# Attention decode on one core: keys as the moving operand on four column tiles, softmax shift and row sums inside the exponential, and a bf16 gather of the output

## The chip, the cores and the metric

The kernel runs on one core of one Trainium2 chip. The metric is the device time of one launch in microseconds (us), and a "median" is taken over several launches. The profile is one profiled launch. Its span, from the first to the last instruction, is about 2 us shorter than the launch's device time. Engines: PE is the TensorE matmul, PEld its weight loads, DVE the VectorE, ACT the ScalarE, POOL the GpSimd, and SP the SyncE, which issues the large loads here.

## The reference, cut to what matters

Two attention layers and two feed-forward layers (FFN) alternate, for 8 sequences with one new token each. Both attention layers read the same cache of 8192 keys and values per head.

```python
B, Sq, D = 8, 1, 512
Hq, Hkv, Sk, Dh = 32, 8, 8192, 128          # 4 query heads share one key/value head
def _A_ref(x, k_cache, v_cache, wq, wo):
    # q = x @ wq by head; k, v repeated 4 times over the heads
    scores = jnp.einsum("bhqd,bhkd->bhqk", q, k) * (Dh ** -0.5)
    p = _softmax(scores, axis=-1)
    o = jnp.einsum("bhqk,bhkd->bhqd", p, v)
    # o, heads side by side, @ wo
...
x = x + _A_ref(_layernorm(x), A_k_cache, A_v_cache, A_wq, A_wo)
x = x + _B_ref(_layernorm(x), B_w1, B_w2)      # silu(h @ w1) @ w2
x = x + _A_ref(_layernorm(x), A_k_cache, A_v_cache, A_wq, A_wo)
x = x + _B_ref(_layernorm(x), B_w1, B_w2)
```

A "unit" below is one layer, one sequence and one key/value head. There are 2 x 8 x 8 = 128 units. A unit needs 8192 keys and 8192 values of 128 numbers, 2 MB each, and serves 4 query rows. K is loaded once for both layers, V once for each layer.

## The kernel before

Sequence by sequence, the kernel runs layer 1 of sequence b together with layer 0 of sequence b + 1, so that loads can go on while the FFN between the layers is computed. All K and V loads go in one fixed order through one queue on SP. V lands in a ring of six 512 KB cells (260 transfers of one cell and 126 of two). K lands in one slot per head. A load waits in the queue until the matmuls that read its buffer's old content are done, and everything behind it waits too.

Every instruction's place is decided when the kernel is built. A small list scheduler in the kernel simulates the program with a duration that the author wrote down for each step. It writes the order that comes out of this simulation into the engines' instruction streams. On the chip each engine then works in that order. Only the semaphores, not the written durations, decide when a step really starts.

```python
class Plan:
    RATE = {1: 2.57, 2: 2.51, 4: 2.48}     # us per MB, by transfer size in cells
    LAND = 2.0                             # us from the end of a transfer to its use
    HOP = 0.1
    PE_SLOW = 1.15
    def add(self, name, eng, dur, emit, prio, deps=()):
        n = Node(name, eng, dur * (self.PE_SLOW if eng == "PE" else 1), emit, prio, deps)
    ...
    def run(self, cells):                  # simulates; a free engine takes its ready step of least prio
    ...
order = plan.run(range(N_CELL - 1))
for n in order:
    n.emit()
```

The scores: each of 64 matmuls per unit loads 128 x 128 numbers of K as the stationary operand and streams 16 columns of queries (`bd`). K was transposed before by DVE (`turns`, four per K slot, in 32-bit pairs).

```python
def score(q=q):
    kv = slot(g).rearrange("p (ck n f e) -> p ck f e n", f=2, ck=NCG, e=2)
    for cg in range(4 * q, 4 * q + 4):
        for fe in range(4):
            pe.matmul(sc[:, 16 * cg:16 * cg + 16], kv[:, cg, fe // 2, fe % 2],
                      bd[:, 16 * fe:16 * fe + 16], start=(fe == 0), stop=(fe == 3))
sn.append(plan.add(f"s{u}.{q}", "PE", 0.56, score, pr - 1, [tn[3], bn] + sn[-1:]))
```

The softmax takes three DVE passes over 256 columns (maximum, subtraction, sum), one ACT exponential, 16 small PE matmuls that turn the result (`swap`) and one ACT copy back from PSUM.

```python
n1 = plan.add(f"mx{u}", "DVE", 0.42, mx, pr - 1, sn)        # maximum of each query row
n2 = plan.add(f"ma{u}", "POOL", 0.45, mall, pr, [n1])       # ... over the partitions
n3 = plan.add(f"sub{u}", "DVE", 0.45, sub, pr - 1, [n2])
n4 = plan.add(f"exp{u}", "ACT", 0.42, exp, pr, [n3] + last_exp)
n5 = plan.add(f"ss{u}", "DVE", 0.42, ssum, pr - 2, [n4])
m4 = plan.add(f"sw{u}", "PE", 0.6, swap, pr - 2, [n4])
n4 = plan.add(f"bk{u}", "ACT", 0.42, back_in, pr, [m4] + p_users.get(sm, []))
```

PV multiplies four probabilities at a time into a 512-column PSUM bank. Four float32 copies and four float32 matmuls (the "gather") then pick the useful blocks and add them up.

```python
for t in range(4):
    k = (NCG * P + 4 * t) * R
    pe.matmul(ot[32 * t:32 * t + 4 * R, :], pt[:, k:k + 4 * R], vt[:, t, :], start=(P == 0), stop=(P == 3))
...
for x in range(4):                                           # take: ACT copy of 128 float32 columns
    pe.matmul(EX[:, 0:R], buf, diag[:, R * x:R * x + R], start=(x == 0), stop=(x == 3))   # float32
    n = plan.add(f"t{u}.{x}", "ACT", 0.3, take, pr - 2, [vs[-1], last])
    es.append(plan.add(f"g{u}.{x}", "PE", 0.25, gather, pr - 2, [n, back(ot_users, 1)]))
```

(These are cuts: the closures and the synchronisation around them are left out.)

## Time and profile before

The kernel took 1256.51 us (median of 3, 1252.25 to 1261.66).

| what, in the profile of the kernel before | value |
|---|---|
| span | 1252.6 us |
| loads | 465 MB in one queue, busy 94.0% of 16 engines' span |
| PE busy | 981.4 us (78%) |
| DVE busy | 526.1 us (42%) |
| the chain that ended last | 59% DMA, 32% PE |

These lines are from the page: the span; each engine's busy time, share and instruction count; the mean busy share of the core's DMA engines in 40 slices, in tenths; the load queue (packets, MB, share of 16 engines' span); and the chain of waits by engine.

```profile
span 1252.6 us, 39642 instructions
PE 981.4 (78%) x17684; PEld 728.5 (58%) x17684; DVE 526.1 (42%) x1196; ACT 240.9 (19%) x859; POOL 117.6 (9%) x299
DMA  9999899999999999999999999999999999999794
...
q1 hardware_dynamic: 86272, 465.10, 94.0%
...
DMA 59%; PE 32%; issue 5%; DVE 1%; SPq 1%; POOL 0%; ACT 0%; POOLq 0%; DVEq 0%
```

The loads bound this kernel, but not perfectly: 6% of the queue's capacity is missing, and a third of the chain is PE. The slices hide where that 6% is, because a slice is 31 us long. The windows view, with shorter stretches, shows it. Its columns are start and end, length, busy time and count of each engine, granted clock, DMA share and GB/s. The clock column can't be read for this kernel: its trace holds no clock record at all, and the view then prints 1.00.

```profile
core 0: us, PE busy (x) PEld busy (x) DVE busy (x) ACT busy (x) POOL busy (x), PEclk, DMA share, GB/s
850.00:875.00 25.00, 25.00 (x447) 18.56 (x440) 7.46 (x23) 5.46 (x20) 2.18 (x5) 1.00 0.91 346
860.00:865.00 5.00, 5.00 (x91) 4.09 (x92) 1.74 (x6) 0.94 (x3) 0.42 (x2) 1.00 0.51 184
```

Around the boundary between the layers PE is full, and inside it the loads run dry (share 0.51). The chain of waits shows what PE does there. Its columns are start, duration, and what ran.

```profile
859.13 0.55 PE sc L725 x16
859.68 0.42 PE ex L844 x2
860.10 0.53 PE sc L725 x16
860.63 0.42 PE ex L844 x2
```

Sixteen score matmuls take turns with one float32 gather matmul (L844; the trace holds two records for each float32 matmul, 1024 for 512): nearly half of PE's time goes to the gather. Next, the view of waits of the SP queue: the queue's line, the engine and line waited for, total us, times, longest.

```profile
SPq L91 <- PE ot L825: 643.7, 309, 20.4
SPq L91 <- PE sc L725: 192.4, 29, 14.3
SPq L91 <- PE yt L894: 70.8, 35, 4.2
```

The queue waits almost only for PE: for PV (which is ordinary back pressure, since V can't come earlier than its ring cell is free), for scores (which free a K slot) and for the output projection. Last, the groups of instructions: line, engine, operation, output and input with shapes, count, then busy us and mean ns of one, then idle time before them with what ended it.

```profile
L725 PE MATMUL sc<-bd,kts 128*128 128x16 bf16 x8192 | 344.7, 182 | 26.1 <-DVE kts L676 17.1 <-DVE bd L710 4.9 <-DVE small L781 2.8
...
L676 DVE STREAM_TRANSPOSE kts<-kts 128x1024 uint32<-128x1024 uint32 x256 | 311.1, 1229 | 94.3 <-DMA kts<-in_A_k_cache_dram 93.9
...
L844 PE MATMUL ex<-diag,p 128*128 128x4 f32 x512 | 147.4, 359 | 9.5 <-ACT p L840 8.6
L844 PE MATMUL ex<-diag,part 128*128 128x4 f32 x512 | 145.5, 355 | 0.0
L844 PEld LDWEIGHTS ex<-diag,part 128*128 128x128 f32 x512 | 138.3, 330 | 0.9 <-issue 0.9
```

The gather costs 293 us of PE busy by these two lines, 2.29 us per unit (259 us where matmuls that overlap count once, my count from the trace), for a reduction of 512 columns to 4. The DVE's K transposes wait 94 us for K to land. A DVE that stands at a transpose can't do a softmax step that is ready behind it.

### The profile page before, as it was taken

The numbers are of one execution on the slowest core, as the hardware profiler recorded it, in microseconds if no ns is written. First come the engines' busy times: TensorE is split into PE (matmuls) and PEld (weight loads), VectorE is DVE, ScalarE is ACT, GpSimd is POOL, SyncE is SP. The second block draws the span as 40 slices with busy tenths as digits, with TensorE's granted clock in tenths as the row PEclk, the third lists the DMA queues.
The fourth block names the chain that finished last, engine by engine and source line by source line (L and its number), as shares of the span: only waits on it lengthen the run. The fifth ranks groups of instructions, "written<-read, shape, count | busy, mean of one in ns | idle before, by whom it ended". The sixth has DMA issues, their size and how long they took to land.

```text
span 1252.6 us, 39642 instructions
## 1 busy us (share of the span) xinstructions
PE 981.4 (78%) x17684; PEld 728.5 (58%) x17684; DVE 526.1 (42%) x1196; ACT 240.9 (19%) x859; POOL 117.6 (9%) x299
## 2 busy tenths in 40 slices
PE   2756787788877978788887987779678896768886
PEld 2545565566665756556665665557456575655664
DVE  5551445415552346514454154723456134651220
ACT  0111111212122112212122121222112121122121
POOL 1000101001010001101010010100011000110010
DMA  9999899999999999999999999999999999999794
GB/s 372 418 402 337 335 400 368 377 355 418 418 389 377 364 417 415 370 383 366 413 398 382 355 375 408 396 382 359 381 412 368 391 362 377 406 372 341 251 352 172
DMA packets 86444, 467.64 MB, mean 373 GB/s; under 512 B 8945, under 2 KB 14849, under 8 KB 61953
## 3 DMA queue, kind: packets, MB, share of 16 engines
q1 hardware_dynamic: 86272, 465.10, 94.0%
q8 instruction: 139, 2.28, 0.7%
q14 instruction: 33, 0.26, 0.1%
HBM read 465.05 MB, written 0.01 MB: 371 GB/s over the span
## 4 chain that ended last, share of the span: by engine, by line
DMA 59%; PE 32%; issue 5%; DVE 1%; SPq 1%; POOL 0%; ACT 0%; POOLq 0%; DVEq 0%
DMA ring<-in_A_v_cache_dram 52%; PE ot L825 11%; PE sc L725 8%; PE ex L844 7%; DMA ring<-in_A_wq_dram 4%; DMA w<-in_B_w_dram 1%; PE misc L625 1%; PE misc L504 1%; SPq L334 1%; PE misc L486 1%; DMA kts<-in_A_wo_dram 1%; PE yt L894 1%; DMA kts<-in_A_k_cache_dram 1%; DVE kts L676 1%; PE sc L762 1%
## 5 line engine op out<-in xcount | busy, mean ns | idle before, releaser
L825 PE MATMUL ot<-ring,p 128*16 128x512 bf16 x2048 | 297.7, 601 | 137.8 <-DMA ring<-in_A_v_cache_dram 137.6
L725 PEld LDWEIGHTS sc<-bd,kts 128*128 128x128 bf16 x8192 | 334.0, 121 | 117.4 <-issue 53.7
L725 PE MATMUL sc<-bd,kts 128*128 128x16 bf16 x8192 | 344.7, 182 | 26.1 <-DVE kts L676 17.1
L676 DVE STREAM_TRANSPOSE kts<-kts 128x1024 uint32<-128x1024 uint32 x256 | 311.1, 1229 | 94.3 <-DMA kts<-in_A_k_cache_dram 93.9
L840 ACT ACTIVATE p<-ot 128x128 f32<-128x128 f32 x256 | 71.0, 277 | 442.1 <-PE ot L825 351.0
L844 PE MATMUL ex<-diag,p 128*128 128x4 f32 x512 | 147.4, 359 | 9.5 <-ACT p L840 8.6
L844 PEld LDWEIGHTS ex<-diag,p 128*128 128x128 f32 x512 | 129.9, 314 | 39.7 <-ACT p L840 25.9
L825 PEld LDWEIGHTS ot<-ring,p 128*16 128x16 bf16 x2048 | 46.2, 90 | 177.6 <-DMA ring<-in_A_v_cache_dram 170.0
L844 PE MATMUL ex<-diag,part 128*128 128x4 f32 x512 | 145.5, 355 | 0.0
L737 DVE TENSOR_REDUCE small<-sc 128x4 f32<-128x256 f32 x128 | 52.7, 411 | 208.4 <-PE sc L725 208.2
L844 PEld LDWEIGHTS ex<-diag,part 128*128 128x128 f32 x512 | 138.3, 330 | 0.9 <-issue 0.9
L742 POOL PARTITION_ALL_REDUCE small<-small x128 | 47.6, 372 | 647.5 <-DVE small L737 473.2
L752 ACT ACTIVATE expd<-sc 128x256 bf16<-128x256 f32 x128 | 49.1, 384 | 301.5 <-DVE sc L747 299.7
L762 PE MATMUL sc<-expd,ident 128*32 128x64 bf16 x2048 | 53.1, 242 | 37.2 <-ACT expd L752 37.1
L777 POOL PARTITION_ALL_REDUCE small<-small x128 | 55.0, 430 | 273.9 <-DVE small L772 230.1
L840 ACT ACTIVATE part<-ot 128x128 f32<-128x128 f32 x256 | 70.3, 275 | 26.5 <-PE ex L844 10.8
L872 DVE TENSOR_TENSOR z<-ex,small 128x16 bf16<-128x16 f32 x64 | 10.8, 168 | 149.1 <-PE ex L865 149.0
L762 PEld LDWEIGHTS sc<-expd,ident 128*32 128x32 bf16 x2048 | 37.6, 123 | 59.4 <-ACT expd L752 50.1
L768 ACT ACTIVATE p<-sc 128x256 bf16<-128x256 f32 x128 | 49.1, 384 | 111.0 <-PE sc L762 110.6
L747 DVE TENSOR_TENSOR sc<-sc,small 128x256 f32<-128x256 f32 x128 | 53.4, 417 | 16.3 <-POOL small L742 16.0
L772 DVE TENSOR_REDUCE small<-expd 128x4 f32<-128x256 bf16 x128 | 50.8, 397 | 19.6 <-ACT expd L752 19.4
L894 PEld LDWEIGHTS yt<-z,ring 128*128 128x128 bf16 x1024 | 32.6, 105 | 20.8 <-issue 19.9
(75 smaller groups left out, 424.4 us busy)
## 6 DMA issues: line engine op xcount, KB each, us to landing
ring<-in_A_v_cache_dram SPq DMA_DIRECT2D x260, 512.0 KB, 7.7
kts<-in_A_k_cache_dram SPq DMA_DIRECT2D x64, 2048.0 KB, 10.6
ring<-in_A_v_cache_dram SPq DMA_DIRECT2D x126, 1024.0 KB, 10.6
ring<-in_A_wo_dram SPq DMA_DIRECT2D x64, 512.0 KB, 11.2
ring<-in_A_wq_dram SPq DMA_DIRECT2D x36, 512.0 KB, 8.0
kts<-in_A_wo_dram SPq DMA_DIRECT2D x2, 2048.0 KB, 14.0
w<-in_B_w_dram SPq DMA_DIRECT2D x2, 1792.0 KB, 13.5
wq<-in_A_wq_dram SPq DMA_DIRECT2D x4, 512.0 KB, 11.1
```

The source lines that it names most:

```text
L676: op(dve, lambda: dve.transpose(v, v), reads=[], writes=[res("kt", g)], add=(q > 0))
L725: steps.append(lambda cg=cg, fe=fe: pe.matmul(sc[:, 16 * cg:16 * cg + 16], kv[:, cg, fe // 2, fe % 2], bd[:, 16 * fe:16 * fe + 16], start= ...
L737: op(dve, lambda: dve.tensor_reduce(mxp[sm], sv.rearrange("p (k h) -> p h k", h=R), AX.X, ALU.max), reads=[res(*scr)], writes=[res("mxp", ...
L747: op(dve, lambda: dve.tensor_tensor(v, v, mxa[sm].unsqueeze(1).to_broadcast([128, NCH, R]), ALU.subtract), reads=[res("mxa", sm)], writes= ...
L752: op(act, lambda: act.activation(pe_out[:, :], sv, ACT.Exp, scale=SM_SCALE), reads=[res(*scr)], writes=[res("expd")])
L762: steps.append(lambda c4=c4, P=P: pe.matmul(new[32 * P:32 * P + 32, c4], ident[:, 32 * c4:32 * c4 + 32], src[:, P], start=True, stop=True))
L768: op(act, lambda: act.activation(pt[:, :], sc[:, 256:512], ACT.Copy), reads=[res(*scr)], writes=[res("p", sm)])
L772: op(dve, lambda: dve.tensor_reduce(ssm[sm], pe_out[:, :].rearrange("p (k h) -> p h k", h=R), AX.X, ALU.add), reads=[res("expd")], writes= ...
L777: op(pool, lambda: pool.partition_all_reduce(ssa[sm], ssm[sm], 128, bass.bass_isa.ReduceOp.add), reads=[res("ssm", sm)], writes=[res("ssa" ...
L825: steps.append(lambda t=t, k=k: pe.matmul(ot[32 * t:32 * t + 4 * R, :], pt[:, k:k + 4 * R], vt[:, t, :], start=(P == 0), stop=(P == 3)))
L840: op(act, lambda: act.activation(buf, ot[:, x * DH:(x + 1) * DH], ACT.Copy), reads=[res("ot", o)], writes=[br])
L844: mms([lambda: pe.matmul(EX[:, 0:R], buf, diag[:, R * x:R * x + R], start=(x == 0), stop=(x == 3))], reads=[br, res("diag")], writes=[res( ...
```

## The change

Its intent is to take work off PE and ACT.

1. Scores: K becomes the moving operand. 32 matmuls of 256 columns, spread over four column tiles of the array (outputs at partitions 0, 32, 64, 96), replace 64 matmuls of 16 columns. The queries become the stationary operand.
2. Softmax: the maximum goes into the exponential as its bias and the row sums come out as its accumulated output. Two DVE passes and a PE turn of 16 matmuls become a PE turn of 4 and one DVE transpose from PSUM.
3. PV: two probabilities at a time, so that only 256 columns are to be gathered. The gather splits them into a bf16 high part and a bf16 remainder (one ACT copy, one DVE subtraction) and uses four bf16 matmuls.
4. The durations that the scheduler is told change along with the instructions. So does the number of buffers for the spread queries (`bd`), from two to one.

The core of the diff, with cuts marked:

```diff
-                kv = slot(g).rearrange("p (ck n f e) -> p ck f e n", f=2, ck=NCG, e=2)
+                kv = slot(g).rearrange("p (c y i f) -> p y f c i", c=8, y=8, f=4)
 ...
-                        steps.append(lambda cg=cg, fe=fe: pe.matmul(
-                            sc[:, 16 * cg:16 * cg + 16], kv[:, cg, fe // 2, fe % 2],
-                            bd[:, 16 * fe:16 * fe + 16], start=(fe == 0), stop=(fe == 3)))
+                        w = bd[:, 48 * q + 16 * (1 - y):48 * q + 16 * (1 - y) + 32]
+                        steps.append(lambda t=t, y=y, w=w: pe.matmul(
+                            sc[32 * t:32 * t + 32, 0:256], w, kv[:, 2 * t + y, q],
+                            start=(q == 0 and y == 0), stop=(q == 3 and y == 1)))
-            sn.append(plan.add(f"s{u}.{q}", "PE", 0.56, score, pr - 1,
+            sn.append(plan.add(f"s{u}.{q}", "PE", 0.3, score, pr - 1,
 ...
-            op(act, lambda: act.activation(pe_out[:, :], sv, ACT.Exp, scale=SM_SCALE),
+            op(act, lambda: act.activation(pe_out[:, :], sv, ACT.Exp, bias=bias[si], scale=SM_SCALE, accum_out=rsum[si]),
 ...
-            op(act, lambda: act.activation(pt[:, :], sc[:, 256:512], ACT.Copy), reads=[res(*scr)],
-               writes=[res("p", sm)])
+            src = sc[:, 256:512].bitcast(BF16).rearrange("p (n two) -> p two n", two=2)[:, 1]
+            op(dve, lambda: dve.transpose(pt[:, :], src), reads=[res(*scr)], writes=[res("p", sm)])
 ...
-        n1 = plan.add(f"mx{u}", "DVE", 0.42, mx, pr - 1, sn)
+        n1 = plan.add(f"mx{u}", "DVE", 0.6, mx, pr - 1, sn + [back(rc_users, N_SC)])
-        n3 = plan.add(f"sub{u}", "DVE", 0.45, sub, pr - 1, [n2])
+        n3 = plan.add(f"own{u}", "DVE", 0.17, own_max, pr - 1, [n2])
-        n5 = plan.add(f"ss{u}", "DVE", 0.42, ssum, pr - 2, [n4])
-        m4 = plan.add(f"sw{u}", "PE", 0.6, swap, pr - 2, [n4])
-        n4 = plan.add(f"bk{u}", "ACT", 0.42, back_in, pr, [m4] + p_users.get(sm, []))
+        n5 = plan.add(f"ss{u}", "DVE", 0.17, ssum, pr - 2, [n4])
+        m4 = plan.add(f"sw{u}", "PE", 0.3, swap, pr - 2, [n4])
+        n4 = plan.add(f"bk{u}", "DVE", 0.45, back_in, pr - 2, [m4] + p_users.get(sm, []))
 ...
-            n = plan.add(f"v{u}.{P}", "PE", 0.4, pv, pr, [h["exp"], vn, old or clear_n] + vs[-1:])
+            n = plan.add(f"v{u}.{P}", "PE", 0.35, pv, pr, [h["exp"], vn, old or clear_n] + vs[-1:])
 ...
-            n = plan.add(f"t{u}.{x}", "ACT", 0.3, take, pr - 2, [vs[-1], last])
-            es.append(plan.add(f"g{u}.{x}", "PE", 0.25, gather, pr - 2, [n, back(ot_users, 1)]))
+        def high():
+            op(act, lambda: act.activation(pt[:, :], ot[:, 0:2 * DH], ACT.Copy), reads=[res("ot", o)],
+               writes=[res("p", sm)])
+        def low():
+            op(dve, lambda: dve.tensor_tensor(part[:, :], ot[:, 0:2 * DH], pt[:, :], ALU.subtract),
+               reads=[res("ot", o), res("p", sm)], writes=[res("part")])
+        def gather():
+            for k, src in enumerate((pt, part)):
+                for y in range(2):
+                    steps.append(lambda k=k, src=src, y=y: pe.matmul(
+                        EX[:, 0:R], src[:, y * DH:y * DH + DH], diag[:, R * y:R * y + R],
+                        start=(k == 0 and y == 0), stop=(k == 1 and y == 1)))
 ...
+        hn = plan.add(f"hi{u}", "ACT", 0.42, high, pr - 2, [vs[-1]])
+        ln = plan.add(f"lo{u}", "DVE", 0.45, low, pr - 2, [hn, back(es, 1)])
+        es.append(plan.add(f"g{u}", "PE", 0.2, gather, pr - 2, [ln, back(ot_users, 1)]))
```

## The prediction

> **What bounds the kernel now.** The loads. The page gives the DMA queue 94% of 16 engines' span, at a mean 373 GB/s; the chain that ended last is 59% DMA, 32% PE. In 25 us stretches (the windows view), undisturbed ones show a DMA share of 1.01 to 1.02 and 412 to 421 GB/s; where V comes in single 512 KB cells, 385 to 394. Dips (0.79 to 0.95) come in each of the eight passes. Summed against 1.015 up to 1175 us they cost 58 us; the end (from 1175 us) loses about 10 more before the last load lands at 1236, then 15 us run without loads. At share 1.01 and the present mix of transfers (373/0.94 = 397 GB/s), I estimate a floor near 1187 us.
>
> **Why the dips.** The queue issues in order and waited almost only for PE (PV 644 us, scores 192, output projection 71). Around the layer boundary PE is full: 25.0 of 25 us at 850:875 and 1000:1025, DMA share 0.91. There a K load waits for the first layer-1 scores, which wait behind float32 gathers and the FFN chain; the loads run dry for 2.5 us (860:865, share 0.51).
>
> **What the change does, per unit of 128.**
> - Gather: four float32 matmuls, with evictions in turn, cost 293/128 = 2.29 us of PE and about that in latency. Four bf16 ones of 4 columns should cost 0.27 us, as the query expansion does; latency about 1.3 us. The Trainium skill, "TensorE: Matmul & The Clock Gate", Weight-path perf modes, says fast weight load excludes FP32; the trace agrees: 314 to 330 ns a load against 104 to 107.
> - Scores: 64 matmuls of 16 columns, 2.3 to 2.7 us, become 32 of 256 on four column tiles. PV streams as many columns (16 of 512) in 4 x 0.43 us, so I estimate 1.7 us. The new operand is strided by 8 bytes; the Trainium skill, "SBUF — State Buffer", Door 1, says two hits per 16-byte line are free. No trace shows that yet.
> - Swap 0.40 to about 0.3 us; PV unchanged.
> - PE busy 981 to about 600 us; ScalarE 241 to about 105.
> - DVE loses passes of 411, 417 and 397 ns, gains a 410 ns maximum, three tiny ones (165 ns), a 400 ns transpose and a 417 ns subtraction: 526 to about 590 us. More of each unit's chain now sits on DVE, behind K transposes of 1229 ns, and DVE waits in order for K to land (94 us).
>
> **Critical path.** PE's 380 us are mostly hidden under the loads. Only the dips (58), the end (10) and the last chain (2) can be won: about 70 us. I expect 55 to 60% of it; the rest stays with in-order K waits on DVE, the FFN chain and single-cell loads.
>
> **Predicted: 1216 us, 1192 to 1240. Chances: faster 0.70, same 0.25, slower 0.05.**
>
> **What would show it.** DMA queue share 96 to 97%; boundary windows at 0.97 or more with PE below 20 of 25 us; four bf16 gathers below 0.35 us; the queue's waits on scores below 120 us; score groups of eight at 0.45 us or less; PE below 20% of the chain.
>
> **What would make it wrong.** Strided streaming at half rate (score groups near 0.8 us); DVE becoming the cause of late releases, so that the dips stay with PE idle; or dips set by the six ring cells and issue order rather than PE, which leaves 1235 to 1250 us. A larger gain would need larger transfers, which don't change.

## The result, and the profile after

The kernel after took **1182.71 us** (median of 4, 1179.12 to 1184.9) against 1254.38 (median of 4, 1251.65 to 1261.66). The ratio is 0.9417, with a 95% interval of 0.9369 to 0.9466. A ratio here is the mean time of one kernel's fast runs over that of the other's fast runs of the same rounds, so it is not quite the ratio of the medians. "Faster" was right; the time lies 9 us below the predicted range.

The page of the kernel after, the same parts as above:

```profile
span 1180.7 us, 31675 instructions
PE 706.9 (60%) x13588; PEld 370.5 (31%) x13588; DVE 597.7 (51%) x1713; ACT 136.9 (12%) x475; POOL 117.3 (10%) x295
DMA  9999799999999999999999999999999999999993
...
q1 hardware_dynamic: 86272, 465.10, 97.8%
...
DMA 76%; PE 16%; issue 4%; DVE 2%; SPq 1%; POOLq 0%; ACT 0%; POOL 0%; DVEq 0%; ACTq 0%
```

The windows view of the kernel after, at the layer boundary and at the very first boundary:

```profile
core 0: us, PE busy (x) PEld busy (x) DVE busy (x) ACT busy (x) POOL busy (x), PEclk, DMA share, GB/s
800.00:825.00 25.00, 20.64 (x454) 11.48 (x454) 6.60 (x28) 3.14 (x11) 1.99 (x4) 0.57 1.02 396
125.00:130.00 5.00, 4.08 (x98) 2.61 (x99) 1.29 (x7) 0.00 (x0) 0.39 (x1) 0.64 0.11 24
```

The later boundaries no longer cost the loads anything: PE is busy 20.64 of 25 us and the DMA share is 1.02. The first boundary still loses them (share 0.11 from 125 to 130 us; the kernel before had 0.03 there). It is the 7 in the slices.

The waits of the SP queue, and the groups, of the kernel after:

```profile
SPq L91 <- PE ot L842: 654.1, 300, 21.5
SPq L91 <- PE sc L746: 155.1, 29, 13.2
SPq L91 <- PE yt L915: 28.6, 17, 3.7
```

```profile
L694 DVE STREAM_TRANSPOSE kts<-kts 128x1024 uint32<-128x1024 uint32 x256 | 306.1, 1222 | 35.4 <-DMA kts<-in_A_k_cache_dram 35.3
L746 PE MATMUL sc<-kts,bd 128*32 128x256 bf16 x4096 | 288.6, 406 | 33.8 <-DVE kts L694 21.7 <-DVE bd L729 8.6 <-DVE rc L796 0.9
...
L772 ACT ACTIVATE expd<-sc,small 128x256 bf16<-128x256 f32 x128 | 60.7, 474 | 422.1 <-DVE small L767 365.6 <-PE sc L746 32.7 <-PE ot L842 17.8
...
L864 PE MATMUL ex<-diag,p 128*128 128x4 bf16 x256 | 26.3, 172 | 23.5 <-DVE part L856 21.2 <-DVE small L767 2.2
L772 ACT ACTIVATION_READ_ACCUMULATOR expd<-sc,small 128x1 f32 x128 | 24.7, 193 | 0.0
L864 PE MATMUL ex<-diag,part 128*128 128x4 bf16 x256 | 24.5, 165 | 0.0
...
L864 PEld LDWEIGHTS ex<-diag,part 128*128 128x128 bf16 x256 | 16.3, 101 | 0.1
```

The gather fell from 293 to 51 us of PE busy (259 to 33 where overlapping matmuls count once), and from float32 weight loads of 330 ns to bf16 ones of 101 ns. This agrees with the Trainium skill, "TensorE: Matmul & The Clock Gate", Weight-path perf modes, which excludes FP32 from the fast weight load. The scores fell only from 345 to 289 us. The exponential grew from 384 to 474 ns, and reading its accumulated sum costs 193 ns more. The DVE works 72 us more, yet waits for K only 35 us instead of 94.

Two quantities organise everything that follows. "Queue busy" is the span times the queue's share. "Queue idle" is the span minus queue busy divided by 1.012. The 1.012 is the share that the page gives when nothing ever holds the loads up (experiment e3 below).

| kernel | span | share | queue busy | queue idle |
|---|---|---|---|---|
| before | 1252.6 | 0.940 | 1177.4 | 89.1 |
| after | 1180.7 | 0.978 | 1154.7 | 39.7 |
| loads only (e3) | 1123.9 | 1.012 | 1137.4 | 0 |

So of the 72 us gained in the profiled span, 49.4 came from a queue that idles less. The other 22.4 (22.7/1.012) came from the *same 86272 packets and 465 MB taking less time*.

### The profile page after: what moved, and what is told of

It is laid out like the page before. It is cut to its first block, busy times and chain, and to the rows that moved or that the text cites. A ratio compares the mean times of both kernels' runs of the same rounds, so it can differ in the third digit from the quotient of the medians.

```text
span 1180.7 us, 31675 instructions
## 1 busy us (share of the span) xinstructions
PE 706.9 (60%) x13588; PEld 370.5 (31%) x13588; DVE 597.7 (51%) x1713; ACT 136.9 (12%) x475; POOL 117.3 (10%) x295
## 3 DMA queue, kind: packets, MB, share of 16 engines
q1 hardware_dynamic: 86272, 465.10, 97.8%
## 4 chain that ended last, share of the span: by engine, by line
DMA 76%; PE 16%; issue 4%; DVE 2%; SPq 1%; POOLq 0%; ACT 0%; POOL 0%; DVEq 0%; ACTq 0%
DMA ring<-in_A_v_cache_dram 70%; PE ot L842 7%; PE sc L746 6%; DMA kts<-in_A_k_cache_dram 3%; DMA ring<-in_A_wq_dram 2%; DMA w<-in_B_w_dram 1%; DVE kts L694 1%; PE misc L642 1%; SPq L340 1%; PE ex L864 0%; PE sc L721 0%; PE yt L915 0%; PE misc L510 0%; DVE small L758 0%; PE ex L886 0%
## 5 line engine op out<-in xcount | busy, mean ns | idle before, releaser
L842 PE MATMUL ot<-ring,p 128*8 128x256 bf16 x4096 | 256.6, 365 | 220.8 <-DMA ring<-in_A_v_cache_dram 218.9
L694 DVE STREAM_TRANSPOSE kts<-kts 128x1024 uint32<-128x1024 uint32 x256 | 306.1, 1222 | 35.4 <-DMA kts<-in_A_k_cache_dram 35.3
L746 PE MATMUL sc<-kts,bd 128*32 128x256 bf16 x4096 | 288.6, 406 | 33.8 <-DVE kts L694 21.7
L842 PEld LDWEIGHTS ot<-ring,p 128*8 128x8 bf16 x4096 | 80.0, 92 | 313.9 <-DMA ring<-in_A_v_cache_dram 288.7
L746 PEld LDWEIGHTS sc<-kts,bd 128*32 128x32 bf16 x4096 | 116.3, 117 | 107.4 <-DVE kts L694 32.1
L856 DVE TENSOR_TENSOR part<-ot,p 128x256 bf16<-128x256 f32 x128 | 54.2, 423 | 177.1 <-ACT p L852 98.5
L772 ACT ACTIVATE expd<-sc,small 128x256 bf16<-128x256 f32 x128 | 60.7, 474 | 422.1 <-DVE small L767 365.6
L852 ACT ACTIVATE p<-ot 128x256 bf16<-128x256 f32 x128 | 49.1, 383 | 487.7 <-PE ot L842 486.7
L778 PE MATMUL sc<-expd,ident 128*32 128x256 bf16 x512 | 42.3, 318 | 91.1 <-ACT expd L772 88.4
L758 DVE TENSOR_REDUCE small<-sc 128x1 f32<-128x256 f32 x128 | 53.2, 415 | 51.3 <-PE sc L746 51.2
L785 DVE STREAM_TRANSPOSE p<-sc 128x256 bf16<-128x256 bf16 x128 | 56.9, 445 | 7.3 <-PE sc L778 4.5
```

The source lines that it names most:

```text
L694: op(dve, lambda: dve.transpose(v, v), reads=[], writes=[res("kt", g)], add=(q > 0))
L746: steps.append(lambda t=t, y=y, w=w: pe.matmul(sc[32 * t:32 * t + 32, 0:256], w, kv[:, 2 * t + y, q], start=(q == 0 and y == 0), stop=(q = ...
L758: op(dve, lambda: dve.tensor_reduce(mxr[si], sv, AX.X, ALU.max), reads=[res(*scr)], writes=[res("mxr", si)])
L772: op(act, lambda: act.activation(pe_out[:, :], sv, ACT.Exp, bias=bias[si], scale=SM_SCALE, accum_out=rsum[si]), reads=[res(*scr), res("bia ...
L778: steps = [lambda P=P: pe.matmul(sc[32 * P:32 * P + 32, 256:512], src[:, P], pe_out[:, :], start=True, stop=True) for P in range(4)]
L785: op(dve, lambda: dve.transpose(pt[:, :], src), reads=[res(*scr)], writes=[res("p", sm)])
```

## The experiments

The theory: the loads bound the kernel, they run dry where PE is too full to free buffers in time, and less PE time closes those dips. Rivals: (A) one part alone, the gather or the scores, makes all of the gain; (B) the gain comes from a different order of the instructions, since the diff also changes the durations that the scheduler is told; (C) the loads have a floor far from the one that I had estimated, so that the sizes don't mean what I took them for. A short name such as "e5" is the first part of a run's label; there is no e8. The diffs are cut to the lines that matter.

### What the loads alone need, and one part at a time

**e1: the kernel after with a float32 gather** (two ACT copies, two float32 matmuls; no subtraction).

```diff
-        hn = plan.add(f"hi{u}", "ACT", 0.42, high, pr - 2, [vs[-1]])
-        ln = plan.add(f"lo{u}", "DVE", 0.45, low, pr - 2, [hn, back(es, 1)])
-        es.append(plan.add(f"g{u}", "PE", 0.2, gather, pr - 2, [ln, back(ot_users, 1)]))
 ...
+                mms([lambda: pe.matmul(EX[:, 0:R], buf, hsum[:, R * y:R * y + R], start=(y == 0), stop=(y == 1))],
+            n = plan.add(f"t{u}.{y}", "ACT", 0.3, take, pr - 2, [vs[-1], back(es, 1) if y else None])
+            ge.append(plan.add(f"g{u}.{y}", "PE", 0.5, gather, pr - 2, [n, back(ot_users, 1)] + ge[-1:]))
```

> The kernel after, with the gather alone undone: two ScalarE evictions and two float32 matmuls (0.57 us each, measured in the kernel before) in place of the two-part bf16 gather (0.4 us for four). It puts back about 0.75 us of PE per unit, 96 us in all (PE busy near 800 us), and takes the 423 ns subtraction off DVE. Theory PE time (what made the loads run dry was a full PE around the layer boundary): 1190 to 1205 us, dips in the boundary windows come back in part. Rival (scores and softmax part made the gain, the gather is idle time): 1180 to 1187 us. Second rival (more work on DVE is what still costs): faster than 1180 us.

Measured: 1202.82 us (1193.59 to 1203.83), ratio 0.9618. The profile fell on its fastest run (PE busy 798 us, queue idle 44). About 20 of the 72 us go back with half of the float32 matmuls.

**e2: the kernel before with a bf16 gather** (two rounds of ACT high part, DVE subtraction and four bf16 matmuls; old scores, old softmax).

```diff
-    diag = sb([128, R * R], FP32, "diag")
+    diag = sb([128, R * R], BF16, "diag")
 ...
+            hn = plan.add(f"hi{u}.{r}", "ACT", 0.42, high, pr - 2, [vs[-1]] + es[-1:])
+            ln = plan.add(f"lo{u}.{r}", "DVE", 0.45, low, pr - 2, [hn, es[-1] if es else back(es_users, 1)])
+            es.append(plan.add(f"g{u}.{r}", "PE", 0.2, gather, pr - 2, [ln, back(ot_users, 1)]))
```

> The kernel before, with the gather alone changed: two rounds of ScalarE high part, DVE subtraction and four bf16 matmuls, in place of four float32 ones. It takes about 1.5 us of PE per unit away (PE busy near 790 us) and adds 0.85 us of DVE per unit (near 635 us), with the scores, the softmax and PV as before. Theory PE time: most of the gain, 1195 to 1220 us. Rival (the gain comes from scores and softmax, or needs both): 1235 to 1256 us.

Measured: 1246.6 us, ratio 0.9987 (0.9959 to 1.0016). This was the first surprise. PE busy fell by 163 us, from 981 to 818, and the time did not move. The queue idled 91 us, as before, and the DVE's wait for K *rose* from 94 to 120 us. Relief of PE is not sufficient.

**e3: the loads only.** Every compute step is left out of the program; only the DMAs are emitted, so the output is zeros and wrong.

```diff
                 for n in order:
-                n.emit()
+                if n.eng == "DMA":
+                    n.emit()
 ...
```

> The kernel after with every instruction of compute left out of the program, so the same 465 MB are loaded in the same order and sizes into the same places, each waiting only for the earlier load into its place; the result is zeros on purpose. It measures the floor that the prediction put at about 1187 us less 15 us of tail. Prediction's floor right: 1165 to 1175 us. Rival (a fuller queue moves more per busy microsecond, so the floor was set too high): 1115 to 1150 us.

Measured: 1125.65 us (two runs, 1125.54 and 1125.76). From its page:

```profile
span 1123.9 us, 637 instructions
...
q1 hardware_dynamic: 86272, 465.10, 101.2%
...
HBM read 465.05 MB, written 0.01 MB: 414 GB/s over the span
```

This is the floor of the loads in this order and these sizes (the kernels before and after issue the same loads in the same order). It lies 61 us below the 1187 that I had estimated; about 15 of these are the tail without loads, which this run doesn't have, and some 46 are a floor set too high. The headroom of the kernel before is at most 1254.38 - 1125.65 = 129 us, not 70; the compute after the last load is in it, and no kernel can win all of that.

### The order of the instructions

**e4: the kernel after, with the scheduler told the old durations.** Only written durations change; each engine executes the same instructions in another order. (The exponential and the subtraction keep theirs, and the new gather is told that it takes as long as the old one.)

```diff
-            sn.append(plan.add(f"s{u}.{q}", "PE", 0.3, score, pr - 1,
+            sn.append(plan.add(f"s{u}.{q}", "PE", 0.56, score, pr - 1,
-        n1 = plan.add(f"mx{u}", "DVE", 0.6, mx, pr - 1, sn + [back(rc_users, N_SC)])
+        n1 = plan.add(f"mx{u}", "DVE", 0.42, mx, pr - 1, sn + [back(rc_users, N_SC)])
-        m4 = plan.add(f"sw{u}", "PE", 0.3, swap, pr - 2, [n4])
+        m4 = plan.add(f"sw{u}", "PE", 0.6, swap, pr - 2, [n4])
 ... (own 0.17 -> 0.45, ss 0.17 -> 0.42, bk 0.45 -> 0.42, rc 0.3 -> 0.18, v 0.35 -> 0.4)
-        hn = plan.add(f"hi{u}", "ACT", 0.42, high, pr - 2, [vs[-1]])
+        hn = plan.add(f"hi{u}", "ACT", 1.2, high, pr - 2, [vs[-1]])
-        es.append(plan.add(f"g{u}", "PE", 0.2, gather, pr - 2, [ln, back(ot_users, 1)]))
+        es.append(plan.add(f"g{u}", "PE", 1.0, gather, pr - 2, [ln, back(ot_users, 1)]))
```

> The kernel after, with the durations that the scheduler assumes set back to those of the kernel before, so that every engine's instruction order is again laid out for slow scores and a slow gather; the instructions themselves are the new ones. Theory PE time: 1178 to 1195 us, within 1% of the kernel after. Rival (the new order of instructions made the gain): above 1215 us.

Measured: 1256.29 us, ratio 1.005 (1.0002 to 1.0098). **The whole gain is gone**, with PE busy at 715 us, nearly as in the kernel after (707). From its profile, the queue's wait for scores and the DVE's wait for K:

```profile
SPq L91 <- PE sc L746: 302.5, 35, 13.4
```

```profile
DVE kts L694 <- DMA kts<-in_A_k_cache_dram: 160.3, 64, 4.4
```

The kernel after had 155.1 and 35.3 in these lines. The windows view (columns as above) and the timeline of e4 show one instance. In the timeline the columns are start, duration, engine, line, operation, operands, count, and in brackets the idle time before and what ended it.

```profile
795.00:800.00 5.00, 1.45 (x28) 0.51 (x24) 2.83 (x5) 0.00 (x0) 0.00 (x0) 0.50 0.92 381
800.00:805.00 5.00, 4.38 (x82) 2.35 (x78) 4.21 (x16) 1.13 (x4) 1.17 (x3) 0.54 0.41 104
```

```profile
795.57 0.62 PE L746 MATMUL sc<-kts,bd 128*32 128x256 bf16 x8
797.26 2.37 DVE L694 STREAM_TRANSPOSE kts<-kts 128x1024 uint32<-128x1024 uint32 x2 [2.17 <-DMA kts<-in_A_k_cache_dram]
799.55 0.19 DVE L729 TENSOR_TENSOR bd<-sc,mask 128x64 bf16<-128x64 f32 x1
799.66 0.41 DVE L758 TENSOR_REDUCE small<-sc 128x1 f32<-128x256 f32 x1
...
799.74 0.59 PE L842 MATMUL ot<-ring,p 128*8 128x256 bf16 x8 [3.55 <-DMA ring<-in_A_v_cache_dram]
...
800.99 1.57 PE L746 MATMUL sc<-kts,bd 128*32 128x256 bf16 x24
...
802.66 0.33 SPq L340 DMA_DIRECT2D kts<-in_A_k_cache_dram  x1
```

The DVE stood 2.17 us at a K transpose whose K had not landed. Behind it, in its fixed order, were the query spread (`bd`) and the maximum, which are short. The scores that read `bd`'s buffer before were done at 795.57 + 0.62 = 796.19, so the spread could have run then; it ran at 799.55. The next unit's scores therefore ended at 800.99 + 1.57 = 802.56, they freed a K slot, the K load was issued at 802.66, and by then the loads had run dry (share 0.41). The profile puts PE's idle 3.55 us before 799.74 down to V, which PE also needed there; but the scores behind could not have started before the spread in any case. This is the harm from in-order DVE waits that the prediction feared, but it depends on the order, not on the new instructions.

**e6: the reverse, the kernel before told short durations for scores, turn, PV and gather.**

```diff
-            sn.append(plan.add(f"s{u}.{q}", "PE", 0.56, score, pr - 1,
+            sn.append(plan.add(f"s{u}.{q}", "PE", 0.3, score, pr - 1,
-        m4 = plan.add(f"sw{u}", "PE", 0.6, swap, pr - 2, [n4])
+        m4 = plan.add(f"sw{u}", "PE", 0.3, swap, pr - 2, [n4])
 ... (v 0.4 -> 0.35, t 0.3 -> 0.2)
-            es.append(plan.add(f"g{u}.{x}", "PE", 0.25, gather, pr - 2, [n, back(ot_users, 1)]))
+            es.append(plan.add(f"g{u}.{x}", "PE", 0.05, gather, pr - 2, [n, back(ot_users, 1)]))
```

> The kernel before, instructions untouched, with the durations that the scheduler assumes shortened to those of the kernel after (scores 0.3, swap 0.3, PV 0.35, gather steps 0.2 and 0.05). Only the order on each engine changes; the order of loads stays. With the fourth run, this completes the square of old and new instructions against old and new order. Theory order: a good part of the 5.8% comes with the order alone, 1200 to 1230 us. Rival, match (the order must fit the instructions, so a mismatch either way costs): 1250 us or slower.

Measured: 1298.06 us, ratio 1.0354 (1.0307 to 1.0401). Slower by 44 us with the old instructions. Its waits view shows the opposite trouble, PE standing at scores for K transposes (17.1 us in the groups of before):

```profile
PE sc L725 <- DVE kts L676: 104.8, 45, 3.8
```

e4 and e6 complete a square:

| | told old or long durations | told short durations |
|---|---|---|
| old instructions | 1254 (before) | 1298 (e6) |
| new instructions | 1256 (e4) | 1183 (after) |

Neither column nor row alone makes the gain. Rival B in its pure form, that an order laid out for short durations is faster by itself, falls as far as e6 tests it: on the old instructions it costs 44 us. (e6 copies the shorter durations only, so its order is not exactly that of the kernel after.) So does my theory in its pure form, that less PE time alone is enough.

**e7: the kernel before with `LAND` (the assumed time from transfer to use) 2.0 -> 4.0**, to see whether the DVE's waits for K in the kernel before can be ordered away by this one number.

```diff
-    LAND = 2.0
+    LAND = 4.0
```

> The kernel before, with one number of the scheduler changed: it assumes that a load lands 4 us after its turn on the queue in place of 2 us, so K transposes stand later in DVE's order. In the kernel before DVE waited 94 us for K to land, in the kernel after 35. Theory head of line (DVE stands at a K transpose while softmax steps behind it are ready): DVE's wait for K below 70 us and 1225 to 1245 us. Rival (PE, not DVE's order, held the kernel before): within 0.5% of 1250 us.

Measured: 1250.94 us, ratio 1.0002 (0.9937 to 1.0067); the DVE's wait for K fell from 94 to 76 us. Nothing gained: this knob doesn't find a better order for the old instructions.

### PE time with the order held still

**e5: the kernel after, each PV matmul issued twice** (the second into unused columns of the bank; the scheduler is not told, so no engine's order changes).

```diff
+                for c in range(2):
+                    for t in range(4):
+                        k = 32 * (2 * P + c) + 8 * t
+                        steps.append(lambda t=t, c=c, k=k: pe.matmul(
+                            ot[32 * t:32 * t + 2 * R, 2 * DH:4 * DH], pt[:, k:k + 2 * R], vt[:, c, t],
+                            start=False, stop=(P == 3 and c == 1), skip_group_check=True))
```

> The kernel after, with each PV matmul issued a second time into the 256 unused columns of its bank, in the order of instructions of the kernel after; the result stays right. It adds about 0.43 us of PE per cell of V, 220 us in all (PE busy near 930 us), to the step that frees a cell. Theory PE time (a full PE makes the loads run dry): at least half of the gain is lost, 1215 us or more. Rival, order (what counts is that DVE's fixed order puts softmax steps ahead of K transposes; PE has room): 1183 to 1200 us.

Measured: 1233.01 us (1229.43 to 1240.84), ratio 0.9846. PE busy rose from 707 to 860 us, and 50 of the 72 us are lost. The queue idles 71 us, and the DVE's wait for K is only 11 us. This is the cleanest proof of the mechanism: same order, same DVE and ACT work, only more PE time. The added time stands in the step that frees a V cell, so e5 doesn't tell a fuller PE from a later release of the cell.

**e10: the same, with the scheduler told** (PV step 0.35 -> 0.7).

```diff
-            n = plan.add(f"v{u}.{P}", "PE", 0.35, pv, pr, [h["exp"], vn, old or clear_n] + vs[-1:])
+            n = plan.add(f"v{u}.{P}", "PE", 0.7, pv, pr, [h["exp"], vn, old or clear_n] + vs[-1:])
```

> The kernel after with each PV matmul issued twice, as in the fifth run (1233 us), but with the scheduler told so (0.7 in place of 0.35 us per PV step). PE busy near 860 us again. Theory match (most of that run's loss was an order laid out for a faster PE): below 1210 us. Rival, PE time (the load itself costs): 1225 us or more.

Measured: 1243.46 us, ratio 0.9941. A scheduler that knows of the added work makes it 10 us worse, not better; one more order, and no larger a step than order alone makes below.

### Less PE time in the kernel before, part by part

**e9: the kernel before, gathering the bf16 high part only** (two ACT copies of 256 columns, four bf16 matmuls, nothing added on DVE; less exact, yet within the tolerance).

```diff
+                op(act, lambda: act.activation(buf[:, :], ot[:, 2 * r * DH:2 * (r + 1) * DH], ACT.Copy),
 ...
+            n = plan.add(f"t{u}.{r}", "ACT", 0.42, take, pr - 2, [vs[-1], back(es_users, 1) if r else None])
+            es.append(plan.add(f"g{u}.{r}", "PE", 0.12, gather, pr - 2, [n, back(ot_users, 1)] + es[-1:]))
```

> The kernel before, with the gather cut to the bf16 high part (two ScalarE evictions of 256 columns, four bf16 matmuls, no subtraction on DVE); less exact on purpose, and the scheduler is told the new durations. It takes about 1.9 us of PE per unit away without adding to DVE, as the second run did (98 us more DVE, no gain). If DVE's added work ate that run's gain: 1205 to 1230 us. If the gather's PE time alone is worth nothing while the scores are slow: 1238 us or slower.

**e11: the kernel before with half of its score matmuls left out** (`fe` 0 and 3 of 0 to 3; a wrong sum, which the tolerance happened to pass).

```diff
-                    for fe in range(4):
+                    for fe in (0, 3):
-            sn.append(plan.add(f"s{u}.{q}", "PE", 0.56, score, pr - 1,
+            sn.append(plan.add(f"s{u}.{q}", "PE", 0.28, score, pr - 1,
```

> The kernel before with half of the score matmuls left out (32 of 64 a unit, wrong result on purpose), scheduler told. PE loses about 1.2 us a unit, on the step that a K load waits for; DVE, ScalarE and the float32 gather are untouched. Theory: the release of K slots by the scores is what holds the loads: 1205 to 1230 us, and the queue's wait for scores falls below 150 us. Rival (softmax and gather decide): 1240 us or slower.

**e12: both cuts, e9 and e11, together** (the edits are the two above; wrong like e11).

> The kernel before with both cuts: high-part gather and half of the scores (wrong result on purpose), scheduler told. PE busy near 640 us, below the kernel after (707), with the old softmax on DVE. If PE time in the right order is the whole cause: 1175 to 1190 us, as the kernel after. If the change of the softmax steps (bias and sums in ScalarE, transpose on DVE) carries part of the gain: 1205 us or slower.

| kernel | median us | ratio (95%) | PE busy | queue idle | queue's wait for scores |
|---|---|---|---|---|---|
| before | 1252.74 | 1 | 981 | 89 | 192 |
| e9, cheap gather | 1205.43 | 0.9636 (0.9605 to 0.9666) | 793 | 51 | 115 |
| e11, half of the scores | 1207.99 | 0.9648 (0.9618 to 0.9679) | 859 | 57 | 54 |
| e12, both | 1187.06 | 0.9501 (0.9449 to 0.9553) | 686 | 42 | 41 |
| after (other rounds) | 1182.71 | 0.9417 (0.9369 to 0.9466) | 707 | 40 | 155 |

Either cut gives 45 to 47 us. Both give 66, not 92: they overlap, because both relieve the same boundary and the loads' floor comes nearer. So rival A finds no support: the better of the two single cuts stays 22 us behind the kernel after. It isn't excluded, since each cut was run in one order and an order alone can be worth 29 us (e16 below). With the old softmax, half of the old scores and 686 us of PE busy, e12 comes within 4 us of the kernel after by the medians (10 by the ratios). As far as this one order shows, the reorganised softmax and the column tiles matter here only as PE time.

### The subtraction on DVE, and the order again

**e13: the kernel after, its DVE subtraction done three times** (the scheduler told 1.35).

```diff
+            for _ in range(3):
+                op(dve, lambda: dve.tensor_tensor(part[:, :], ot[:, 0:2 * DH], pt[:, :], ALU.subtract),
 ...
-        ln = plan.add(f"lo{u}", "DVE", 0.45, low, pr - 2, [hn, back(es, 1)])
+        ln = plan.add(f"lo{u}", "DVE", 1.35, low, pr - 2, [hn, back(es, 1)])
```

> The kernel after with the subtraction on DVE issued three times in a row (same result), scheduler told. It adds about 0.85 us of DVE per unit, 108 us in all (DVE busy near 705 us), inside the gather's chain; PE is untouched. Theory DVE in the chain (what ate the gain of the second run, bf16 gather in the kernel before, was its 98 us more DVE): 1205 us or more. Rival (DVE has room, that run failed because slow scores filled PE): 1183 to 1195 us.

Measured: 1189.72 us, ratio 0.9496. The DVE is busy 698 instead of 598 us, and this costs 7 us by the medians (10 by the ratios). As far as this one order shows, DVE time is nearly free here.

**e14: the kernel after without the subtraction** (high part only; less exact).

```diff
-            for k, src in enumerate((pt, part)):
+            for k, src in enumerate((pt,)):
 ...
-        ln = plan.add(f"lo{u}", "DVE", 0.45, low, pr - 2, [hn, back(es, 1)])
-        es.append(plan.add(f"g{u}", "PE", 0.2, gather, pr - 2, [ln, back(ot_users, 1)]))
+        es.append(plan.add(f"g{u}", "PE", 0.2, gather, pr - 2, [hn, back(ot_users, 1)]))
```

> The kernel after with the high part alone in the gather, no subtraction on DVE (less exact on purpose), scheduler told. DVE falls by 54 us, the chain from PV to the normalisation by about 0.5 us. It measures what the exact two-part gather costs in the kernel after. Theory DVE in the chain: 1165 to 1178 us. Rival (hidden under the loads): 1178 to 1186 us.

Measured: 1195.5 us, ratio 0.9538. Strictly less work than the kernel after, and 13 us *slower*. Removing a step also moves every later step in the order, so an ablation in this kernel carries an error of at least this size.

**e15: the kernel before, half of the scores and the full bf16 gather of e2** (the edits of e11 and e2; wrong).

> The kernel before with half of the score matmuls left out (wrong result on purpose) and the exact bf16 gather of the second run, scheduler told. The run with half scores alone took 1208 us, half scores with the high part alone 1187 us. If DVE's 98 us eat what the gather gives: 1205 us or more. If the bf16 gather pays once the scores are short: 1183 to 1198 us.

Measured: 1193.99 us, ratio 0.9529 (0.949 to 0.9569), against 1187 for e12. With the scores cut, the gather that gave nothing in e2 gives 14 us (1207.99 to 1193.99).

**e16 and e17: exactly the instructions of e2, with the subtraction's written duration changed from 0.45 to 0.2 and to 0.7.** They answer what was still open: whether e2's missing gain was the DVE subtraction itself, or only an unlucky order.

```diff
-            ln = plan.add(f"lo{u}.{r}", "DVE", 0.45, low, pr - 2, [hn, es[-1] if es else back(es_users, 1)])
+            ln = plan.add(f"lo{u}.{r}", "DVE", 0.2, low, pr - 2, [hn, es[-1] if es else back(es_users, 1)])
```

> The second run's instructions (kernel before with the exact bf16 gather), unchanged, in another order: the scheduler is told 0.2 us for the subtraction in place of 0.45. If that run's missing gain was its order, one of this pair lies at 1200 to 1225 us; if DVE's added work ate it whatever the order, both lie within 1% of 1246 us.

> The same instructions as the run beside it in a third order: the scheduler is told 0.7 us for the subtraction. Same expectations: 1200 to 1225 us if the order decided the second run, within 1% of 1246 us if DVE's added work did. The spread of the three orders is also the measure of how far any single run of this study can be off by its order alone.

Measured: e16 1217.76 us, ratio 0.9733 (0.9706 to 0.9759); e17 1224.57, ratio 0.9785 (0.9756 to 0.9814). All three kernels have 818 us of PE busy and 620 to 624 us of DVE busy, and their times are 1246.6, 1217.8 and 1224.6. So 22 to 29 us of e2's missing gain was the order it happened to get (25 to 32 by the ratios, since e2 is of other rounds). The bf16 gather alone is worth between nothing clear of noise (3 us, e2) and 34 us in the kernel before, depending on nothing but the order. The sum of the DVE's waits for K doesn't tell a good order from a bad one here: it is 120 us in e2, 119 in e16, 112 in e17, and 131 in e9, which gained 47 us.

### Two attempts to beat the kernel after

**v1: load the FFN weights before the last unit's V in the first pass**, against the dip at the first boundary.

```diff
+            if b < 0 and i == len(vs) - 1:
+                load_ffn()
 ...
-        if b < 0:
-            load_ffn()
```

> The kernel after, with the two FFN weight loads (3.6 MB) issued before the last two V loads of the first pass in place of after them. In the kernel after, the first FFN waits for them and the loads run dry at 125 to 130 us (DMA share 0.11). Expected 2 to 5 us faster than the kernel after; if the dip only moves, no change.

Measured: 1194.63 us, ratio 0.9525. The dip got deeper: the fifth slice of the page moved 194 GB/s instead of 311. A miss.

**v2: tell the scheduler the durations that the trace of the kernel after shows** (scores 0.45, own 0.25, exponential 0.66, sum 0.22, PV 0.37, gather 0.25; those of PE are the measured ones divided by the scheduler's factor `PE_SLOW`, 1.15).

```diff
-            sn.append(plan.add(f"s{u}.{q}", "PE", 0.3, score, pr - 1,
+            sn.append(plan.add(f"s{u}.{q}", "PE", 0.45, score, pr - 1,
-        n4 = plan.add(f"exp{u}", "ACT", 0.42, exp, pr, [n3] + last_exp)
+        n4 = plan.add(f"exp{u}", "ACT", 0.66, exp, pr, [n3] + last_exp)
 ... (own, ss, v and g likewise)
```

> The kernel after, with the scheduler's assumed durations set to those measured in its own trace (score step 0.52, exp with its accumulator read 0.66, own maximum 0.25, PV step 0.43, gather 0.29 us, PE values divided by the scheduler's 1.15). Only the order on the engines changes. The fourth run shows that an order laid out for the wrong durations costs 73 us; if the right ones help, 1165 to 1180 us; if the order is good enough as it stands, 1180 to 1186 us.

Measured: 1199.13 us, ratio 0.9573. Truer durations gave an order that is 16 us worse, with the DVE's wait for K at 89 us instead of 35. A miss, and a lesson: the scheduler's model leaves out enough that the written durations act as tuning knobs, not as facts. No run beat the kernel after.

## Why the prediction was right or wrong

**Right: the mechanism.** The loads bound the kernel, and they ran dry where PE was full. e5 shows this with the order held still: 154 us more PE busy take back 50 us. e9 and e12 show it from the other side, each in one order. The gather was right: its four bf16 matmuls at one place of the trace run from 795.88 to 796.14, 0.26 us, where I had said 0.27; over all 128 units the mean is 0.26 as well. DVE busy (597.7, predicted about 590), the share of the chain on PE (16%, predicted under 20), PE in the boundary (20.64 of 25 us, predicted under 20: narrowly missed) and the DMA share there (1.02) came out about as written. The queue's share came out at 97.8%, above the predicted 96 to 97.

**The step that failed: "Only the dips (58), the end (10) and the last chain (2) can be won: about 70 us."** This term was mis-sized. I had multiplied a share of 1.01 by a rate of "397 GB/s" that was itself measured in a kernel that stalls, and so got a floor "near 1187 us". The loads-only run, which has no tail of compute, takes 1125.65. The headroom of the kernel before is at most 129 us, and it has two parts:

| term | predicted | headroom measured | recovered by the change |
|---|---|---|---|
| queue idle | 70 | 89.1 | 49.4 (55%) |
| time of the same packets | 0 | 39.5 = (1177.4 - 1137.4)/1.012 | 22.4 (57%) |
| together | 70 | 128.6 | 71.9 (56%) |

I had expected to win about 40 us of the 70 and won 71.9. The larger part of the miss, 22.4 us, is the second row, which I had not in the sum at all. The other 9.4 are in the first row: 49.4 us are 71% of the 70. (The 70 leaves out 13 of the 15 us without loads at the end. With them I had counted 83 us of idle queue, near the 89.1 measured.) That all fractions of the measured headroom lie near the 55 to 60% that I had named is luck. By place (my own count from the packet records), the queue's idle time fell from 52.4 to 7.9 us between 150 us after the start and 75 us before the end, where the dips are, but only from 12.8 to 12.0 in the first 150 us and from 24.3 to 20.2 in the last 75. So 85% of the idle time in the later dips was won, and very little of that at the start and the end.

The second row means that a packet's time is not constant. In the packet records of the traces (my own count, packets of 1 KB and more in the load queue), the median 4 KB packet takes 159 ns before and after and 161 in the loads-only run. But 2932 packets of the kernel before took over 1.5 times the median of their size, against 1397 after and 148 in the loads-only run. Their time above the median is 50.3, 25.0 and 2.8 us of the 16 engines, so they cover the 22.7 us of queue busy that fell away. In 5 us stretches with a DMA share below 0.95, or next to one, this excess fell from 27.1 to 7.4 us; elsewhere, from 23.2 to 17.5. In the kernel before, 4 KB packets that start within 1 us after a full gap in the traffic take 363 ns on average against 170 otherwise, but these are only 241 packets. Queue busy above the 1137.4 of e3 is 0.45 of the idle time before and 0.44 after, and 0.57, 0.35 and 0.54 of it in e1, e2 and e5. So closing a dip seems to pay for the dip and again for slow packets in and beside it. This is a correlation over the runs. The amount of the engines' own traffic doesn't set it alone: e4 runs the instructions of the kernel after and has a queue busy of 1179.7 against 1154.7, and e13, with 100 us more DVE work, has 1155.2. *Why* packets are slower near a dip, and why some are slow elsewhere, stays open.

**Wrong: "the rest stays with in-order K waits on DVE".** The DVE's wait for K fell to 35 us, and e13's 100 us of further DVE work cost 7 to 10 us. The rest that stayed, 40 us of idle queue, is largely elsewhere: 20.2 us in the last 75, where the loads end, 12.0 in the first 150, and 7.9 in all the stages between.

**Wrong in size, without consequence for the time.** "I estimate 1.7 us" for a unit's scores and "score groups of eight at 0.45 us or less": the scores took 288.6/128 = 2.25 us of PE busy per unit. In the e4 timeline above 8 such matmuls took 0.62 us and 24 took 1.57, so each further eight cost (1.57 - 0.62)/2 = 0.47 us, close to the expected 0.45; what I had left out is the start and end that each separate group pays. My estimate came from PV, and here a second thing was hidden. By the clock records of the kernel after (my own count, groups that lie wholly in one state of the clock), PV's 8 and 16 matmuls take 0.60 and 1.03 us at a granted clock of 0.50, and 0.41 and 0.61 at 1.00. So each further eight cost 0.43 and 0.205. The scores take 0.63 and 1.11 (0.50), and 0.63 and 1.09 (1.00; medians): 0.46 to 0.48 for each further eight at either clock. At the lower clock they are nearly as fast as PV, and at the full clock they take over twice as long for as many columns. These lines of the kernel after, a window, sixteen score matmuls and sixteen of PV, show it at one place:

```profile
768.00:773.00 5.00, 3.60 (x72) 1.80 (x72) 4.25 (x15) 0.56 (x2) 1.18 (x3) 1.00 1.02 419
```

```profile
769.60 1.09 PE L746 MATMUL sc<-kts,bd 128*32 128x256 bf16 x16
...
772.02 0.61 PE L842 MATMUL ot<-ring,p 128*8 128x256 bf16 x16 [0.40 <-DMA ring<-in_A_v_cache_dram]
```

The Trainium skill, "SBUF — State Buffer", Door 1, asks for two hits per 16-byte line for full bandwidth, which the 8-byte stride of K gives. No run here confirms that this makes the stride free: the half rate that I had named as a risk is what the scores show at the full clock, measured against PV. Whether the stride causes it, or the wider weights (32 against 8 columns) that are loaded for every matmul, was not tested. PE busy came out at 707 rather than 600 us. ACT came out at 137 rather than 105: I had not costed the slower exponential and its 193 ns accumulator read, which together are 36 us. The queue's wait for scores stayed at 155 us where I had said under 120. Times waited in a queue that is full anyway are poor witnesses: e13 with 190 us is faster than e9 with 115.

**Not considered: the order.** The prediction treated the diff's written durations as bookkeeping. They are half of the change. With the old durations the same instructions take 1256 us (e4). Order alone moves identical instructions by 29 us (e2, e16) and by 16 and 74 us (v2, e4). That the author's durations fit the new instructions is part of why the change works, and I had no term for it. Nor had I one for the clock that TensorE is granted. All runs with the old scores have no clock record, and PV in the kernel before takes 0.60 us or more for each four matmuls of 512 columns (1.03 for eight), as at 0.50 in the kernel after. All runs with the new scores have records (0.68 of full clock on average after). So PV fell from 297.7 to 256.6 us of PE busy, where I had written "PV unchanged". That this isn't needed for the gain is shown by e12: 1187 us with PV at 300.1. Because of the order, the share of each part can't be given to better than some 30 us (e2 against e16): 45 to 47 us for each cut in the kernel before, 3 to 34 for the bf16 gather with its subtraction, 20 for half of the float32 gather in the kernel after. Which order would be best stays open.

## What to carry to other kernels

Where loads bound a kernel, measure the floor with a loads-only run instead of scaling a rate taken from a kernel that stalls: here a stall went along with slower packets in and around it, and so cost more than its own length. Where a scheduler fixes the order from written durations, a changed duration is a change of the program: test new instructions in the old order and old instructions in the new one before crediting either. Repeat an ablation under a second order, because one order's luck was worth 30 us and more here.

## What the Trainium skill lacked or had wrong

- "SBUF — State Buffer", Summary: rules for kernel authors, advises about 358 GB/s for transfers from HBM. One core alone moved 414 GB/s over the whole span of the loads-only run. "DMA: Bandwidth & Descriptors", Bandwidth, gives 425 GB/s for 16 MB with the other core idle, and this is the nearer figure here.
- No page has it: packets are slower where the traffic dips. The packets that took over 1.5 times their median cost 50.3 us before, 25.0 after and 2.8 without stalls, most of the difference in and beside dips (27.1 us before, 7.4 after), and the same 465 MB took 1177, 1155 and 1137 us of queue time.
- "TensorE: Matmul & The Clock Gate", Part 1, says that an idle TensorE falls to half its clock and that matmuls then take about twice as long. For PV this agrees (0.43 against 0.205 us for each further eight matmuls), but not for the scores, whose operand is strided and whose weights are wider: 0.47 at either clock. The lines show PV at a granted clock of 0.50 after, and in the kernel before, without a clock record, with as many streamed columns:

```profile
849.49 1.03 PE L825 MATMUL ot<-ring,p 128*16 128x512 bf16 x8
```

```profile
1151.19 1.02 PE L842 MATMUL ot<-ring,p 128*8 128x256 bf16 x16 [1.88 <-DMA ring<-in_A_v_cache_dram]
```

- "TensorEngine Tiling (Array Packing)" and Part 3 of the TensorE page give speedups of one packed set, but no sustained rate. Here four column tiles of 512 columns came every 0.43 us in the kernel before. In the kernel after eight matmuls of 256 columns came every 0.43 us (granted clock 0.50) or 0.205 (1.00) with 8-column weights, and every 0.47 us at either clock with 32-column weights and the strided operand.
- "ScalarE: Activation LUTs" says that an activation can give an accumulator output, without the cost of reading it: 193 ns here.
